# Linear attention feeding a gated causal convolution: a new instruction order, two more batches through the DMA crossbar, one load on another queue

## The chip, the cores and the metric

The kernel runs on one core of a Trainium2 chip. TensorE (PE), VectorE (DVE), ScalarE (ACT), GpSimd (POOL) and SyncE (SP) each work through their own list of instructions in order, and wait for one another by semaphores. SP computes nothing here; it issues DMAs. POOL computes and issues DMAs as well. The metric is the device time of one execution, in microseconds (us).

## The reference: what is computed

There are 8 batches, 8 heads, 576 positions and 64 features per head. With w_phi of 64 x 128:

```
phi(x): proj = x @ w_phi;  proj -= max|proj| over features;  [exp(proj), exp(-proj)]
kv = phi(k)^T v        z = sum over positions of phi(k)
x  = (phi(q) kv) / (phi(q) z + 1e-6)          heads side by side: 8 x 576 x 512
gate = sigmoid(causal convolution of x with 5 taps per channel)
out  = (gate * (x @ w_val)) @ w_out
```

## The kernel before

**Stages of a batch b.** The names below are the methods of the class Emit, and each of them is one task of the plan.

1. Load: `load` brings q and k of batch b as bf16 into one pair of tiles (KQN) that all batches from 2 on share. It is issued by POOL, q before k. `loadv` (line 504) brings v in fp32, issued by SP. Batch 0 comes in fp32 in nine pieces on SP (`load32`).
2. Transpose to features by rows: `xpose` (line 536) is a DMA transpose through the crossbar, issued by SP, for k and for q from batch 2 on. Batches 0 and 1 go through TensorE (`tp32`, `tp16`) and are copied out of PSUM by DVE or ACT.
3. k side: `kp` projects (PE), `kmax` takes the maxima (DVE), `kexp` the exponentials (ACT), `ek` the exponentials of the maxima (ACT), `vs` scales v by them (POOL, or DVE), `st` forms kv and z (PE), `kv` copies them out (DVE or ACT).
4. q side: `qm` projects for the maxima (PE), `qmax` (DVE), `mqt` and `mqr` transpose the maxima (PE, DVE), `rx` spreads them over a small identity (POOL, or DVE), `qp` projects again and adds them (PE), `qexp` (ACT).
5. `num` multiplies by kv (PE), `nrm` divides (DVE) into XN. The result is then transposed into XT: by 8 PE transposes (`xtp`, line 695) and a DVE copy (`xtc`, line 709) for each of two blocks, or, for the batches in `XB`, by a DMA transpose (`xtd`, line 706) that SP issues. A third, small block goes through PE always. `halo` (POOL) copies the positions that the convolution reaches back to.
6. `gate` (PE), `tanh` (ACT), `val` (PE), `gv` (DVE), `gvc` (POOL), `out` (PE), `oev` (ACT or DVE) and `odma` (SP).

q and k of batch 0 are kept in the second KTIL buffer and q and k of batch 1 in the second QTIL buffer, so the profile calls these transfers KTIL<-in_q_dram, QTIL<-in_q_dram and the like.

**What sets the order.** `build` lists 1,089 tasks with their dependencies. The kernel does no scheduling of its own: `ORDER` is a written-out table of task numbers, and each engine's instructions follow that table. `FLEX` names the engine of every task that has a choice, `BANKS` the PSUM banks. `WARM` puts dummy matmuls at given places of the order. Since every engine works in order, a task that waits holds up all that stands behind it on its engine. Two small POOL copies are there only to wait: `hold` keeps the loads of batch 1 back until a piece of batch 0 has landed, and `holdx` keeps the loads of batch b+2 back until the transposed q of batch b+1 has landed, since the KQN tiles are free only then.

**Queues.** SP issues, in order, the loads of batch 0, all v loads, one copy of the second half of w_val (`c_dup`, line 448), the transposes of k and q, the transposes of XN for the batches in XB, and the output. POOL issues the q and k loads and the weights. Both kinds of queue share the same 16 DMA engines.

Of the kernel before, what the change touches and what calls it, by code (L numbers as in the profile page):

```python
# [16 lines left out]
B, H, S, D = 8, 8, 576, 64  # L17
F = 128
DM = 512
P = 128  # L20
# [6 lines left out]
XB = (6, 7)  # L27
# [6 lines left out]
    "81:2:1 156:4:2 "  # L34
# [6 lines left out]
    "0 1 2 9 3 4 11 5 6 10 42 13 7 8 44 20 21 12 46 47 22 23 24 25 45 26 27 28 29 40 41 183 184 30 14 32 31 33 43 180 50 19 "  # L41
    "181 76 160 161 36 49 34 48 37 74 51 77 80 162 163 52 75 164 165 35 15 38 53 16 39 78 62 17 81 79 306 307 54 166 167 82 "
    "83 18 58 182 84 57 59 85 102 176 56 174 90 60 177 61 103 91 105 104 178 55 179 308 309 86 220 92 93 94 87 88 98 170 221 "
    "99 89 175 222 101 171 168 172 223 63 216 64 100 217 173 169 65 197 218 224 225 200 95 199 219 96 97 70 66 67 185 310 311 "
    "201 187 198 188 203 189 68 190 204 226 227 69 192 186 202 228 71 191 72 240 229 232 193 73 230 194 112 114 231 196 205 "
    "108 195 113 241 115 106 243 244 242 116 118 109 236 233 234 107 235 207 117 316 206 119 317 110 312 313 332 318 319 120 "
    "121 433 111 208 434 435 351 122 209 126 314 315 333 334 352 127 347 335 320 210 128 322 323 129 436 437 353 130 438 439 "
    "348 123 131 124 125 354 237 238 355 349 321 324 326 327 356 139 212 350 357 239 140 328 331 330 358 211 325 213 245 246 "
    "247 440 441 214 132 215 329 133 367 141 368 371 134 248 359 375 369 363 254 142 249 370 360 361 260 250 362 255 261 256 "
    "442 443 364 462 251 137 336 366 257 463 135 365 138 136 454 464 337 262 444 445 567 465 252 450 456 263 568 569 485 253 "  # L50
    "148 258 457 486 570 571 264 455 453 338 149 259 452 144 152 376 274 145 275 153 377 265 378 266 479 451 276 458 154 155 "
    "480 267 461 339 483 340 460 268 269 341 484 271 272 459 481 482 572 573 270 477 446 273 156 342 343 344 345 478 487 488 "
    "489 449 372 157 448 346 277 490 373 447 283 574 575 146 147 278 501 374 493 381 497 498 491 505 695 492 284 466 578 281 "
    "500 382 579 499 279 282 280 385 386 696 697 581 391 698 699 580 506 609 392 610 158 159 507 494 508 576 577 150 151 495 "
    "379 468 380 393 615 394 467 616 472 286 496 582 473 287 387 388 469 613 614 470 585 584 502 471 583 617 618 389 504 395 "
    "290 383 700 701 390 384 503 611 612 590 702 703 291 474 593 475 476 592 399 400 594 619 401 285 294 517 591 597 620 586 "
    "518 295 596 595 625 396 397 405 406 621 408 588 398 511 637 587 407 589 706 629 633 709 708 409 521 515 512 402 403 404 "
    "522 296 297 827 292 293 516 288 289 598 143 704 705 509 707 638 410 630 640 510 639 631 411 828 829 745 523 632 302 741 "
    "303 746 622 830 831 414 605 524 604 722 742 412 415 623 723 606 624 743 607 832 833 725 413 724 626 525 608 627 634 628 "
    "600 744 739 298 740 599 513 714 636 299 514 601 635 834 835 416 602 715 737 603 429 738 710 716 519 747 300 301 425 717 "  # L60
    "711 641 748 520 421 955 430 713 712 647 642 718 532 533 422 653 721 648 529 426 530 654 534 526 535 536 720 527 531 537 "
    "544 304 305 854 528 753 719 545 749 726 857 765 856 423 424 655 754 755 540 956 957 431 432 656 766 768 767 733 855 538 "
    "958 959 541 756 750 427 428 752 649 539 757 643 728 650 644 657 542 543 727 758 875 751 876 761 759 842 651 652 732 845 "
    "760 551 873 547 417 552 645 843 874 871 548 844 762 729 418 730 764 836 837 646 846 872 734 735 763 731 869 658 659 847 "
    "849 660 736 877 848 870 838 667 668 781 669 878 839 879 771 546 777 960 961 782 772 563 880 775 778 885 840 841 564 850 "
    "661 662 664 665 852 776 783 663 559 666 419 420 853 881 962 963 882 784 553 554 884 560 670 672 851 886 883 889 671 1005 "
    "673 674 1006 982 858 888 676 887 890 984 549 550 675 897 769 677 865 779 683 985 891 785 892 983 964 965 898 565 566 900 "
    "770 974 773 977 684 860 774 555 685 686 687 899 864 556 893 780 975 1001 557 558 795 688 796 786 1002 976 787 997 797 "
    "789 790 999 788 998 791 970 1003 1000 859 1004 792 973 793 794 972 800 966 969 679 1007 801 861 968 862 678 971 1008 798 "
    "967 863 680 894 978 561 562 802 895 799 1025 979 1009 1013 804 1021 896 803 805 1010 866 981 867 807 868 903 986 980 907 "  # L70
    "913 806 1011 1012 808 681 682 988 904 1022 1017 914 1023 992 1026 1027 915 908 691 916 987 909 823 993 689 690 1028 901 "
    "1024 809 810 692 910 994 1014 824 902 995 1016 1018 989 990 1015 819 1019 991 811 1020 996 1031 905 906 1035 693 694 "
    "1029 812 820 1032 917 815 1030 911 912 1037 927 1041 1036 928 924 1038 925 825 826 1042 921 1039 1040 929 1033 1034 922 "
    "1043 816 918 919 926 1044 930 920 936 932 813 814 923 931 1045 1049 933 1052 1055 1050 937 1046 1051 1047 1056 821 822 "
    "1053 1064 1048 934 1057 817 818 1062 1065 1060 935 1058 1054 943 1063 939 940 947 1059 1061 1067 1071 1079 951 1066 1075 "
    "938 944 945 946 948 941 942 1068 1083 1080 949 950 1072 1076 1084 1069 1070 1073 1074 1081 1082 1087 1088 952 953 954 "
    "1077 1078 1085 1086 "
)
FLEX = (
    "DDAAAAAAAAPPDPPDPDPPDDAAADDDDDDPPDPPDPPPPPAAADAPPAPPAPPPPDADDAPPAPPDPDPPPAAADDPPAPPAPPPPPADAAPPAPPDPPPPPADDADPPAPPDPPPPP"  # L80
    "ADDDPPDPDDPPPPPAAADA"
)
BANKS = (
    "616077010145236745674545234523450124567670101236704523011012367454523670102107662331012301236767014501012345567672345236"
    "723345453620167012301012345177032345456745232301010123670016723676723014672362067456745236767454012454567450101676767230"
    "101123456723012367101453226723670101236723762644545010123674567236767016016745230145015234570423674567016745014111456745"
    "452323010145670101023674567454501301670400167672301234501076602323452301234567010101015452323236745456767102301452345236"
    "7675427670145676745234523674501523670123452301450177670145236701230103162"
)


# [66 lines left out]
def build(plan, em=None):  # L158
# [7 lines left out]
    A = plan.add  # L166
    h = {}
    seq, oseq = [], {}

    def G(*k):  # L170
        return h.get(k)
# [690 lines left out]
```

## Time and profile before

| what | value |
|---|---|
| median of 3 runs | 227.13 us (225.67 to 228.78) |
| the profiled execution's own time | 227.83 us |
| its span, first to last instruction | 226.1 us |
| PE busy | 195.4 us (86%) |
| DVE, ACT, POOL busy | 177.4, 178.6, 136.8 us |
| DMA packets | 39.83 MB, mean 176 GB/s |
| TensorE clock granted, mean of the span | 0.985 |

The profile page cuts the span into 40 slices of about 5.65 us and gives each engine's busy share in tenths. Further views are the chain of work that ended last, the waits (who waited for whom), timelines of one engine, and windows (busy time between two points). Landing times of single DMAs are read from the trace's DMA completions. A wait is put down to the thing that came last.

### The profile page before, as it was taken

To read this page: it belongs to the slowest core of one execution; us is meant where nothing else is said; L and a number is where in the kernel's file an instruction comes from. 1 tells how busy PE (TensorE), PEld (TensorE's weight loads), DVE (VectorE), ACT (ScalarE), POOL (GpSimd) and SP (SyncE) were. 2 spreads that over 40 slices of the span, in tenths; PEclk is the share of its full clock that TensorE was granted. 3 is DMA by queue.
4 is the path that set the end of the run, shared out by engine and by line. 5 is a ranking of instruction groups with operands and counts; after the bars stand their busy time and mean duration, and the time that the engine had idled before them with its cause. 6 is when DMAs were issued, how large, how long until landed. Compare 5 with 4: busy or idle time off the path is not lost.

```text
span 226.1 us, 8730 instructions
## 1 busy us (share of the span) xinstructions
PE 195.4 (86%) x3768; PEld 141.2 (62%) x3787; DVE 177.4 (78%) x272; ACT 178.6 (79%) x264; POOL 136.8 (61%) x196
## 2 busy tenths in 40 slices
PE   3697677788979999889999998889999999899990
PEld 2474446566656766567776875566766867687630
DVE  3589999988978989977989878778988967653640
ACT  2599999989989999769999998868999997243230
POOL 4589988896279278928893089906693796010200
PEclk9979999999999999999999999999999999999997
DMA  6999986999989599949995979879932311954085
GB/s 219 292 277 283 215 171 110 243 210 174 130 217 246 119 173 264 253 76 181 255 259 106 161 218 232 213 114 203 259 100 83 96 46 40 154 102 138 0 249 169
DMA packets 49424, 39.83 MB, mean 176 GB/s; under 512 B 33706, under 2 KB 38826, under 8 KB 49322
## 3 DMA queue, kind: packets, MB, share of 16 engines
q1 hardware_dynamic: 43136, 29.63, 55.4%
q0 software_dynamic: 5760, 9.31, 23.1%
q8 instruction: 29, 0.48, 0.8%
q10 hardware_dynamic: 490, 0.35, 0.5%
q14 instruction: 9, 0.07, 0.1%
HBM read 30.49 MB, written 9.44 MB: 177 GB/s over the span
## 4 chain that ended last, share of the span: by engine, by line
PE 57%; DMA 14%; DVE 9%; POOL 8%; ACT 5%; issue 4%; SPq 0%; DVEq 0%; POOLq 0%; ACTq 0%
PE PS L775 12%; PE PS L751 10%; PE PS L594 7%; PE PS L733 6%; PE PS L551 6%; DMA qT<-KQN 6%; DVE MQP L558 4%; PE PS L671 4%; POOL VT L584 4%; POOL RX L637 3%; DMA kT<-KQN 3%; PE PS L739 3%; DMA KTIL<-in_q_dram 3%; DVE MK L558 2%; PE PS L700 2%
## 5 line engine op out<-in xcount | busy, mean ns | idle before, releaser
L568 ACT ACTIVATE KTIL<-PS 128x1024 bf16<-128x1024 f32 (+1 forms) x80 | 72.2, 967 | 4.9 <-PE PS L551 3.2
L584 POOL TENSOR_TENSOR VT<-VN,EK 128x1152 bf16<-128x1152 f32 x31 | 65.8, 2122 | 7.9 <-ACT EK L577 6.8
L658 ACT ACTIVATE QTIL<-PS 128x1024 bf16<-128x1024 f32 x64 | 62.4, 1052 | 4.3 <-PE PS L650 4.2
L637 POOL TENSOR_TENSOR RX<-MQR,ident 128x512 bf16<-128x512 bf16 (+1 forms) x36 | 34.5, 986 | 25.3 <-DVE MQR L630 18.4
L558 DVE TENSOR_REDUCE MK<-PS 128x8 f32<-128x1024 f32 (+1 forms) x40 | 44.3, 1112 | 5.0 <-PE PS L551 3.8
L558 DVE TENSOR_REDUCE MQP<-PS 128x8 f32<-128x1024 f32 (+1 forms) x40 | 43.6, 1112 | 4.0 <-PE PS L551 2.4
L751 PE MATMUL PS<-XT,WV 64*128 64x288 bf16 x512 | 35.1, 283 | 0.2 <-DVE MQP L558 0.2
L743 ACT ACTIVATE TH<-PS 128x576 bf16<-128x576 f32 x32 | 20.4, 661 | 16.7 <-PE PS L739 13.0
L757 DVE SCALAR_TENSOR_TENSOR GV<-TH,PS 128x576 bf16<-128x576 bf16 x32 | 23.8, 751 | 10.6 <-PE PS L751 8.1
L775 PE MATMUL PS<-WOUT,GV 128*128 128x512 bf16 x112 | 29.5, 380 | 1.0 <-issue 0.2
L751 PEld LDWEIGHTS <-WV 64*128 64x128 bf16 x512 | 25.1, 94 | 7.3 <-issue 2.2
L594 PE MATMUL PS<-VT,KTIL 64*128 64x65 bf16 x1152 | 23.2, 191 | 4.7 <-issue 2.8
L594 PEld LDWEIGHTS <-KTIL 64*128 64x128 bf16 x1152 | 21.0, 94 | 8.3 <-issue 5.0
L692 DVE TENSOR_TENSOR XN<-PS,RCP 128x512 bf16<-128x512 f32 x32 | 22.1, 692 | 2.2 <-DMA XT<-XN 1.1
L733 PE MATMUL PS<-XT,GF 128*64 128x288 bf16 x256 | 21.2, 289 | 1.9 <-issue 1.0
L671 PEld LDWEIGHTS <-QTIL 128*128 128x128 bf16 x512 | 17.8, 97 | 6.5 <-issue 4.0
L671 PE MATMUL PS<-KV,QTIL 128*128 128x65 bf16 x512 | 19.8, 194 | 0.8 <-ACT QTIL L658 0.8
L551 PE MATMUL PS<-W,kT 64*128 64x128 bf16 x288 | 15.2, 223 | 4.0 <-DMA kT<-KQN 1.4
L775 PEld LDWEIGHTS <-GV 128*128 128x128 bf16 x128 | 11.3, 98 | 11.4 <-issue 0.2
L608 ACT ACTIVATE OUTS<-PS 128x512 f32<-128x512 f32 x21 | 12.6, 613 | 5.4 <-PE PS L775 5.3
L551 PE MATMUL PS<-W,qT 64*128 64x128 bf16 x288 | 15.0, 219 | 2.0 <-ACT QTIL L658 0.8
L733 PEld LDWEIGHTS <-GF 128*64 128x64 bf16 x256 | 13.6, 109 | 4.4 <-issue 2.6
(77 smaller groups left out, 256.2 us busy)
## 6 DMA issues: line engine op xcount, KB each, us to landing
VN<-in_v_dram SPq DMA_DIRECT2D x8, 1152.0 KB, 8.3
out_dram<-OUTS SPq DMA_DIRECT2D x31, 256.0 KB, 3.2
KQN<-in_q_dram POOLq DMA_DIRECT2D x6, 576.0 KB, 8.9
KQN<-in_k_dram POOLq DMA_DIRECT2D x6, 576.0 KB, 11.9
KTIL<-in_k_dram SPq DMA_DIRECT2D x4, 288.0 KB, 4.0
KTIL<-in_q_dram SPq DMA_DIRECT2D x4, 256.0 KB, 5.8
out_dram<-OUTS SPq DMA_DIRECT2D x14, 64.0 KB, 2.7
QTIL<-in_q_dram POOLq DMA_DIRECT2D x1, 576.0 KB, 9.7
```

Source lines behind the costliest of these rows:

```text
L551: nc.tensor.matmul(self.PS[:, t.grp.banks[par], i * P:(i + 1) * P], X[rows, (c0 + i) * P:(c0 + i + 1) * P], self.W2[rows, :], start=True, ...
L558: self.nc.vector.tensor_reduce(o, self.two(t.grp, n * P).rearrange("p a (c f) -> p a c f", f=F), AX.X, ALU.max, apply_absolute_value=True)
L568: self.nc.scalar.activation(self.KTIL[b % 2][:, s, c0:c0 + n, :, :].rearrange("p c a f -> p a c f"), self.two(t.grp, n * P).rearrange("p a ...
L584: eng.tensor_tensor(self.VT[g][:, s, :, 0:D], self.VN[b % 2][:, NC * g:NC * g + NC, :], e.to_broadcast([P, NC, D]), ALU.mult)
L594: nc.tensor.matmul(self.PS[:, t.grp.banks[ab], (s * 2 + x) * E1:(s * 2 + x + 1) * E1], self.KTIL[b % 2][rows, s, J // 2, J % 2, :], self.V ...
L637: eng.tensor_tensor(self.RX[u][:, :, 0:n, :], m, e, ALU.mult)
L658: self.nc.scalar.activation(o, i, AF.Exp, scale=1.0 - 2.0 * s)
L671: nc.tensor.matmul(self.PS[:, t.grp.banks[h // 4], (h % 4) * E1:(h % 4 + 1) * E1], Q[:, s, c % 2, h, (c // 2) * P:(c // 2 + 1) * P], self. ...
L733: self.nc.tensor.matmul(self.PS[h2 * D:(h2 + 1) * D, t.grp.banks[par], 0:R], self.GF[:, h, i, :], X[:, h, :, HALO - 8 * s:HALO - 8 * s + X ...
L751: nc.tensor.matmul(self.PS[:, t.grp.banks[par], 0:R], self.WV2[rows, h, j * P:(j + 1) * P], X[rows, h, :, HALO:XW], start=(h == 0), stop=( ...
L757: nc.vector.scalar_tensor_tensor(out=self.GV[b % 3][:, j, :, :], in0=self.TH[j][:, :, :], scalar=1.0, in1=self.two(t.grp, R), op0=ALU.add, ...
L775: nc.tensor.matmul(self.PS[:, t.grp.banks[0], :], lhsT, self.WOUT[:, j, :], start=(j == 0), stop=(j == 3))
```

## The change

The diff has six parts.

1. `ORDER`, `FLEX` and `BANKS` are new tables (the planner that wrote them, which is no part of the kernel, took its transfer times from landings).
2. `XB` is (4, 5, 6, 7) where it was (6, 7): four more blocks of XN go through `xtd` on SP and no longer through `xtp` on PE and `xtc` on DVE. The dependency that made all `xtd` wait for the last k and q loads is gone.
3. `loadv` of batch 1 is issued by POOL, after the q and k loads and w_val; it was the second v load on SP, next to that of batch 0.
4. `hold` waits for the fifth piece of q of batch 0 (`HOLDU`); it waited for the fourth piece of k.
5. `WARM` places 1, 3 and 1 dummy matmuls where it placed 1 and 2.
6. By the new table POOL has 32 of the 40 `rx` (36 before) and 30 of the 32 `vs` (31 before); DVE has the others. DVE has 10 of the 16 `kv` (9 before) and 16 of the 36 `oev` that can go either way (14 before).

```
-XB = (6, 7)
+XB = (4, 5, 6, 7)
+HOLDU = 4
-    "81:2:1 156:4:2 "
+    "76:6:1 80:7:3 128:6:1 "
...
+                if w == "q":
+                    hold = [None, A("lk", b, 0, "POOL", 0.15, fn("hold", HOLDU), [lds[HOLDU]], rank=-600)]
...
-                if w == "k":
-                    hold = [None, A("lk", 0, 0, "POOL", 0.15, fn("hold", 3), [lds[3]], rank=-600)]
...
-        ld = h["lv0",] = A("lv", b, 0, "SP", 0.65, fn("loadv", b),
+        ld = h["lv0",] = A("lv", b, 0, "POOL" if b == 1 else "SP", 0.65, fn("loadv", b),
...
-                    xt = h["xtp", b, i] = A("xtp", b, i, "SP", 1.4, fn("xtd", b, i), nrms + war + [G("xf", B - 1)], lat=-0.2)
+                    xt = h["xtp", b, i] = A("xtp", b, i, "SP", 1.4, fn("xtd", b, i), nrms + war, lat=-0.2)
...
     def hold(self, t, u):
-        self.nc.gpsimd.tensor_copy(self.HOLD[:, :], self.XN32["k"][:, u * 9 * D:u * 9 * D + 1])
+        c = UNITS[u][0] * P
+        self.nc.gpsimd.tensor_copy(self.HOLD[:, :], self.XN32["q"][:, c:c + 1])
...
     def loadv(self, t, b):
-        self.nc.sync.dma_start(self.VN[b % 2][:, :, :].rearrange("p (hp j) d -> p hp (j d)", hp=4), self.rows("v", b))
+        eng = self.nc.gpsimd if t.eng == "POOL" else self.nc.sync
+        eng.dma_start(self.VN[b % 2][:, :, :].rearrange("p (hp j) d -> p hp (j d)", hp=4), self.rows("v", b))
```

The tables, decoded into task names, put the queues so at the places that matter (left before, right after; a number behind a name is the batch, then the unit):

```
POOL, start   hold, loadq1, loadk1, c_wv, loadq2, c_gt, loadk2, rx0 x3, vs0 x4, rx1 x5
         ->   hold, loadq1, loadk1, c_wv, loadq2, loadk2, loadv1, vs0, rx0 x2, vs0 x2, c_gt, rx1 x3
POOL, b 2     rx1 x5, vs1 x2, holdx2, c_wo, halo0, loadq3, loadk3, vs1 x2
         ->   rx1 x3, vs1 x2, holdx2, c_wo, loadq3, loadk3, halo0, rx1, vs1 x2, rx1
POOL, b 5     holdx6, rx5 x3, loadq7, vs5, loadk7, rx5, vs5, halo4, vs5, rx5, vs5
         ->   rx5 x2, holdx6, loadq7, rx5, loadk7, vs5 x3, gvc2, halo4, vs5     (two rx5 on DVE)
SP, start     loadv0, loadv1, c_dup, xposek2, xposeq2, loadv2
         ->   loadv0, xposek2, c_dup, xposeq2, loadv2
SP, b 4       odma1 x2, odma2 x3, loadv6, xposek7, odma2, xposeq7, odma3 x2, loadv7
         ->   odma1, odma2, odma1, xtd4, odma0, xtd4, xposek7, odma2, loadv6, odma2, xposeq7,
              odma3, xtd5, odma3, xtd5, odma2, loadv7
```

`c_gt` is the set-up of the convolution's weights, 16 POOL instructions; `c_wv` and `c_wo` load w_val and w_out.

## The prediction

> **What bounds the kernel now.** I read the page's busy times and slices first, then windows of 50 us, then the waits, and last the chain of work over the one stretch where it leaves TensorE for long. The page:
>
> ```profile
> PE 195.4 (86%) x3768; PEld 141.2 (62%) x3787; DVE 177.4 (78%) x272; ACT 178.6 (79%) x264; POOL 136.8 (61%) x196
> ...
> PE   3697677788979999889999998889999999899990
> ...
> DVE  3589999988978989977989878778988967653640
> ACT  2599999989989999769999998868999997243230
> ...
> DMA  6999986999989599949995979879932311954085
> ```
>
> PE is at seven tenths for the first eight slices (45 us), with DVE and ACT at nine; then it is at eight or nine tenths to the end. The windows put figures on the three bounds:
>
> ```profile
> 12.00:32.00 20.00, 15.95 (x262) 10.63 (x258) 19.23 (x24) 19.55 (x32) 19.73 (x27) 0.94 1.11 249
> ...
> 50.00:100.00 50.00, 44.54 (x967) 32.24 (x971) 44.08 (x65) 46.50 (x69) 32.84 (x40) 1.00 0.93 188
> 100.00:150.00 50.00, 46.65 (x948) 34.27 (x953) 41.76 (x63) 43.28 (x66) 33.09 (x48) 1.00 0.93 189
> 150.00:200.00 50.00, 48.17 (x979) 35.85 (x988) 41.21 (x71) 40.38 (x60) 28.40 (x36) 1.00 0.55 121
> ```
>
> (Columns: window, length, busy PE, PEld, DVE, ACT, POOL, granted clock, DMA share, GB/s.) From 12 to 32 us DVE and ACT leave 0.8 and 0.5 us of 20 unused: they set the pace, beside DMA engines that are full (1.11). From 50 to 200 us PE works 139.4 of 150 us, so 10.6 us is all that a better order can win there without taking work off PE. The DMA engines are nearly as full (0.93) until 150 us. The waits say why:
>
> ```profile
> SPq L539 <- DMA KQN<-in_k_dram: 67.5, 6, 15.6
> ...
> POOL HOLD L487 <- DMA qT<-KQN: 14.6, 5, 10.3
> ```
>
> Each of the six `xposek` waited for k to land. The cycle is: hold released, load q and k (12 us), transpose both (9 us), hold released again; the holds end at 44.8, 65.8, 85.6, 108.2 and 130.8 us, a period of 20 to 23 us, as long as PE needs for a batch. Where this cycle is late it shows in the chain of work:
>
> ```profile
> 124.77 5.89 DMA qT<-KQN
> ...
> 130.78 0.19 POOL HOLD L487
> ...
> 144.07 2.08 POOL VT L584
> ...
> 146.41 0.80 PE PS L594 x39
> ```
>
> POOL idled 10.31 us at this hold with all five `rx` of batch 5 behind it, then worked without a break until 146.4 us, and PE got the last `st` of batch 5 only then.
>
> **The change, part by part.** The sum is made against the profiled execution (227.83 us, span 226.1), 0.70 us above the median of 227.13; I take 0.7 off at the end.
>
> *Crossbar for batches 4 and 5.* Off PE go 4 blocks of 8 transposes. The group of such transposes is 7.4 us for 96, so 32 are 2.5 us; back to back a block takes 0.55 us in the chain. PE loses 4 x 0.55 = 2.2 us of work between 135 and 167 us, where it is 95% busy: **-2.2**. Off DVE go 4 copies of 0.685 us; DVE is not the bound there (41 of 50 us), so 0. On SP come 4 issues of 1.3 us; the queue has room, it waits 67 us in all. The new wait: each `xtd` waits for `nrm`, and behind it on SP stand `odma0`, `xposek7`, `loadv6`, `xposeq7`. Batch 4's last `nrm` ended at 136.9 us and `xposek7` could start only at 147.8, so these hold up nothing. Batch 5's have `loadv7` behind them, issued at 156.8 and first used after 181: covered. What is late next is `gate`. A transpose of XN landed 3.3 to 5.0 us after issue (median 4.1) with no loads beside it, and `nrm` is done 1.3 us after its `num` (163.64 to 164.92), which makes 5.4 us. In the new order the PE work between the last `num4` and the first `gate4` is two `qp` (0.6 each), four projections (0.35), three `out` (0.81) and half of `st5` (1.26): 6.3 us. Between the last `num5` and `gate5` it is 5.6 us. So quiet transposes would just fit; beside q and k of batch 7 the row nearest in kind is `xpose` beside loads, 6.3 to 6.8 us to landing with 2.25 times the bytes. Each of two batches may stall PE by 0 (4.1 us to landing) to 2.2 us (6.8 us: 8.1 against 5.9 of cover): **+1.5**, between 0 and +4.4, nearer to the small transposes' own row.
>
> *POOL in batch 5.* Two `rx5` now stand ahead of the hold, two more on DVE, and only one behind it. With the hold at the same time, the stretch from 130.8 to 146.4 us (5 `rx` of 1.04, 4 `vs` of 2.12 plus 0.27, 2 loads, a halo) loses 4 x 1.04 us and gains a `gvc` of 0.78: `st5` could come 3.4 us sooner. PE's own gaps from 138 to 151 us (0.58, 0.45, 0.52, 0.47, 0.59) are all there is to win, 2.6 us. I take half, **-1.3**, between -2.6 and 0, since DVE gets two `rx` (0.76 each) there.
>
> A row speaks against this part. When DVE did the one `vs` that it has (186.13 us, 1.44 us long), the small POOL cast beside it took 1.40 us in place of 0.26. The Trainium skill, page "SBUF — State Buffer" (section on practical consequences), has the rule: a DVE instruction with two SBUF inputs shuts out a GpSimd instruction that reads SBUF for its whole length. The trace agrees with it in that row. By it each `rx` or `vs` moved to DVE stops POOL while it runs, the two `rx5` cost POOL 1.5 of the 3.4 us, and the sum would be some 0.6 us higher.
>
> *Start.* Without v1 and batch 1 beside them the pieces of q0 follow k0 (landed at 7.0 us) at the rate of those first slices, 300 GB/s: 1.18 MB in 3.9 us. The second piece, which came at 10.17 us and cost ACT its 1.49 us idle, comes at about 8.7: -1.5. The hold now ends near 11 us where it ended at 7.05, and behind it on POOL are all seven loads. But the DMA engines have v0 to bring until 14 us, so they do not run dry. Nine tensors of 1.18 MB or nearly so took them from 3 to 33 us, 3.4 us each; k2, now the eighth of the nine and no longer the last, should land near 33 us where it landed at 35.2 (3 us, eight times 3.4, and some 2 us for stragglers), and v1 near 36, with `vs1` wanting it at 39.2. `c_dup` (7.0 us to landing) moves behind `xposek2`, to 44 us, before its first use at 51.9. So the first hold of the cycle ends 1 to 2 us sooner; `halo0`, now behind `c_wo` and two loads (0.8 + 0.5 + 0.75 us), eats that. `c_gt` (7.8 us of POOL) moves behind three `vs0` and is first needed by `gate0` at 46. Against it: DVE takes one `vs0` (1.44 + 0.27), one `rx0` (0.76) and two small copies (0.42 each) and gives up three of 0.7: +1.2 us; ACT takes a copy of 0.6, one like 0.97 and a `kv` of 0.61 for two of 0.42: +1.3 us. Both are full there, so these count: -1.5 + 1.3 and a little of the sooner hold, **-0.5**, between -3 (copies hidden, hold 2 us sooner and used) and +2 (q1 late by the later hold). Two more dummy matmuls (0.38 us each) lie in PE's idle time: 0; cover gone, +0.8.
>
> *The rest of the table.* Nearly every engine's list is permuted. Its planned ties can win some of the other 8 us of PE gaps or add as much; nothing in the trace prices it: 0, between -2.5 and +2.5. The tail (34 `out` matmuls, 7.5 us, then the last outputs) has the same work in another order: 0.
>
> Sum: -2.2 + 1.5 - 1.3 - 0.5 = -2.5, so 225.3 against the profiled execution and **224.6 us** against the median, 1.1% faster.
>
> **Rivals.**
> (a) *The cycle of loads becomes the bound at batch 7: slower.* Two `xtd4` now fall into the loads of q7 and k7, and `loadv6` moves from ahead of `xposek7` to between `xposek7` and `xposeq7`. From 189 to 198 us two transposes and five outputs took 6.8 us of DMA time; about 2 of it is outputs, so a transpose costs up to 2.4 us. Two of them and v6's 3.5 us ahead of `xposeq7` put its landing from 158.65 to 167 us. Its first use, `qm7`, ran at 160.24, and all of PE stands behind it: from 160.24 on each us is lost, 6.7 us. With -2.2 kept, and the 0.7: 227.83 + 4.5 - 0.7 = 231.6. I call it **232**. For it: DMA share near 1 from 128 to 144 us, only 1.6 us of slack. Against it: v6 leaves that stretch, which should bring k7 sooner by what the transposes cost.
> (b) *The order is simply better: faster.* The gates are not late, the 2.6 us at batch 5 and the 1.5 us at the start come in full with the copies hidden: -2.2 - 2.6 - 1.5 = -6.3, **220.8 us**. For it: POOL's stretch is real; against it, the cover of 5.6 to 6.3 us is no longer than the chain of 5.4.
> (c) *It does not do what it says*: v1 still shares all 16 engines, the gates take back the 2.2 us, and one wait replaces another: **227 us**. For it: the windows show DMA above 0.9 whatever queue issues. The Trainium skill, page "DMA: Bandwidth & Descriptors" (section "Issuing engines are not separate DMA queues"), says that too; the trace agrees, as q1's queue and POOL's ran together at a share of 1.11.
>
> **Chances.** Forecast 0.50, (a) 0.20, (b) 0.18, (c) 0.12. About 2% (4.5 us: 222.6 to 231.7) is what a measurement of this kernel can tell from no change; its three runs spread over 1.4%. Of the forecast's own range, 221.5 to 228, a tenth lies below 222.6, and of (b) nine tenths: 0.21 faster. Of (a) some nine tenths lie above 231.7: 0.18 slower. Within 2%: 0.61. The range for 8 in 10 takes in most of (a) and (b): 220.5 to 232.
>
> **What would show it.** In the profile after: 64 and not 96 transposes at the xtp line; `gate4` and `gate5` idle for XT<-XN by less than 2 us each; the hold of batch 6 with little idle time of `st5` behind it; ACT's wait of 1.49 us near 10.9 us gone; the first `xposek` before 35 us; `qm7` not waiting for qT. A long wait of PE for qT or kT in batches 6 or 7, or for XT, would make me wrong on the slow side; a PE share of 89% or more, on the fast side.

## The result, and the profile after

The changed kernel takes **237.7 us** (median; 236.57 to 241.85). The kernel before, run beside it on the same chip, takes 226.49. The ratio is 1.0462, with a 95% interval of 1.0352 to 1.0571: about 10.5 us slower. Medians here and below are of all executions of a version, while a ratio leaves out those that came out some per cent slow, and is against the kernel before timed beside that version. I had forecast 224.6 us, in a range from 220.5 to 232.

The profiled execution took 237.26 us with a span of 235.5. Its page, the same rows as before:

```profile
PE 198.8 (84%) x3739; PEld 140.5 (60%) x3757; DVE 193.1 (82%) x276; ACT 178.9 (76%) x262; POOL 134.9 (57%) x191
...
PE   3978576899998979999999908989999999899990
...
DVE  2799999899899899998999995879888889662641
...
PEclk9999979999999999999999965999999999999997
DMA  6999999796999899799959690799846036377076
```

PE has a zero in slice 24, from 135.4 to 141.3 us, where it had an eight or nine before; the clock that it is granted falls to 6 there and to 5 in the next slice. DVE is busy 15.7 us longer than before (177.4 to 193.1), although four copies of 0.685 us were taken from it. The windows, with the columns of those before (window, length, busy PE, PEld, DVE, ACT, POOL, granted clock, DMA share, GB/s):

```profile
12.00:32.00 20.00, 13.70 (x176) 8.73 (x177) 19.75 (x26) 18.40 (x30) 19.23 (x28) 0.98 1.12 233
50.00:100.00 50.00, 45.76 (x953) 32.61 (x957) 46.11 (x67) 46.43 (x70) 35.87 (x47) 1.00 0.94 186
100.00:150.00 50.00, 41.75 (x794) 30.26 (x792) 44.40 (x60) 36.47 (x56) 31.44 (x42) 0.90 0.78 157
150.00:200.00 50.00, 47.97 (x969) 33.26 (x976) 43.39 (x63) 44.06 (x65) 26.10 (x33) 1.00 0.68 157
```

Between 12 and 32 us PE does 2.3 us less work than before, and from 100 to 150 us 4.9 us less. The second is the larger loss, and the chain of work has it in one piece (start, length, what):

```profile
131.31 0.60 DVE RX L641
...
133.04 0.99 DVE RX L641
134.03 7.36 issue
141.38 0.75 DVE GV L761
142.18 0.40 PE PS L649 x2
...
142.78 1.92 PE PS L755 x16
```

A small DVE instruction, then 7.36 us in which DVE waits for nothing that the profile shows, then work goes on. The last row is a `val` group of 16 matmuls: 1.92 us instead of the 0.98 that such a group takes elsewhere in this chain, at the low clock after the stall (0.50 from 141.3 to 147.2 us). What DVE did in that time stands in its timeline (start, length, engine, line, operation, out<-in):

```profile
131.22 0.68 DVE L641 TENSOR_TENSOR RX<-MQR,ident 128x512 bf16<-128x512 bf16 x1
...
133.04 8.42 DVE L641 TENSOR_TENSOR RX<-MQR,ident 128x256 bf16<-128x256 bf16 x1
141.38 1.41 DVE L761 SCALAR_TENSOR_TENSOR GV<-TH,PS 128x576 bf16<-128x576 bf16 x2
```

The first row is `rx5,1`, the second `rx5,4`: half as large and twelve times as long. `rx` is the operation for which both inputs lie in SBUF. GpSimd beside it:

```profile
132.18 0.61 POOL L528 DMA_DIRECT2D KQN<-in_q_dram  x1 [0.22 <-issue]
132.81 1.05 POOL L641 TENSOR_TENSOR RX<-MQR,ident 128x512 bf16<-128x512 bf16 x1
133.80 0.81 POOL L528 DMA_DIRECT2D KQN<-in_k_dram  x1
134.63 2.13 POOL L588 TENSOR_TENSOR VT<-VN,EK 128x1152 bf16<-128x1152 f32 x1
136.69 0.27 POOL L589 CAST VT<-EK 128x18 bf16<-128x18 f32 x1
136.85 2.12 POOL L588 TENSOR_TENSOR VT<-VN,EK 128x1152 bf16<-128x1152 f32 x1
138.91 0.25 POOL L589 CAST VT<-EK 128x18 bf16<-128x18 f32 x1
139.07 2.11 POOL L588 TENSOR_TENSOR VT<-VN,EK 128x1152 bf16<-128x1152 f32 x1
141.13 0.45 POOL L589 CAST VT<-EK 128x18 bf16<-128x18 f32 x1
```

GpSimd works without a break through the loads of batch 7, one `rx` and three `vs` of batch 5. Only its last cast is longer than its fellows (0.45 against 0.26), and there `rx5,4` ends. So it looks as if DVE had been shut out by seven GpSimd instructions in a row. The waits about the load cycle, on which I had spent most of my worry, are not longer than before (of SyncE's six `xposek`, four wait last for k where all six did):

```profile
SPq L543 <- DMA KQN<-in_k_dram: 53.1, 4, 21.5
...
POOL HOLD L490 <- DMA qT<-KQN: 9.8, 2, 6.3
```

For the transposes of XN PE waits 0.2 us in all in this profile, once, at 213.5 us.

### The profile page after: what moved, and what is told of

Its sections match the earlier page's. It is cut to its first block, busy times and chain, and to the rows that moved or that the text cites. A ratio compares the mean times of both kernels' runs of the same rounds, so it can differ in the third digit from the quotient of the medians.

```text
span 235.5 us, 8674 instructions
## 1 busy us (share of the span) xinstructions
PE 198.8 (84%) x3739; PEld 140.5 (60%) x3757; DVE 193.1 (82%) x276; ACT 178.9 (76%) x262; POOL 134.9 (57%) x191
## 4 chain that ended last, share of the span: by engine, by line
PE 52%; DVE 22%; issue 8%; ACT 8%; DMA 7%; SPq 1%; DVEq 0%
PE PS L779 11%; PE PS L755 9%; PE PS L598 6%; PE PS L555 5%; PE PS L737 5%; PE PS L675 5%; ACT KTIL L572 4%; DVE MK L562 4%; DVE MQP L562 4%; DMA kT<-KQN 3%; DVE XN L696 3%; DVE RX L641 2%; PE PS L649 2%; PE PS L743 2%; DMA KTIL<-in_k_dram 2%
## 5 line engine op out<-in xcount | busy, mean ns | idle before, releaser
L588 POOL TENSOR_TENSOR VT<-VN,EK 128x1152 bf16<-128x1152 f32 x30 | 64.3, 2143 | 4.8 <-ACT EK L581 4.7
L641 POOL TENSOR_TENSOR RX<-MQR,ident 128x512 bf16<-128x512 bf16 (+1 forms) x32 | 31.0, 990 | 41.3 <-DVE MQR L634 26.3
L755 PE MATMUL PS<-XT,WV 64*128 64x288 bf16 x512 | 36.7, 290 | 0.1
L755 PEld LDWEIGHTS <-WV 64*128 64x128 bf16 x512 | 25.8, 96 | 7.3 <-issue 1.0
L675 PEld LDWEIGHTS <-QTIL 128*128 128x128 bf16 x512 | 18.5, 98 | 8.2 <-issue 6.4
L649 PE MATMUL PS<-qT,W 64*128 64x512 bf16 (+1 forms) x80 | 15.4, 368 | 8.0 <-DVE GV L761 7.1
L675 PE MATMUL PS<-KV,QTIL 128*128 128x65 bf16 x512 | 20.6, 195 | 1.6 <-DVE KV L606 1.0
L555 PE MATMUL PS<-W,qT 64*128 64x128 bf16 x288 | 15.5, 222 | 4.4 <-ACT KTIL L572 1.7
L779 PEld LDWEIGHTS <-GV 128*128 128x128 bf16 x128 | 11.3, 97 | 12.8 <-issue 1.7
```

Of the source, the lines that this page charges most:

```text
L555: nc.tensor.matmul(self.PS[:, t.grp.banks[par], i * P:(i + 1) * P], X[rows, (c0 + i) * P:(c0 + i + 1) * P], self.W2[rows, :], start=True, ...
L588: eng.tensor_tensor(self.VT[g][:, s, :, 0:D], self.VN[b % 2][:, NC * g:NC * g + NC, :], e.to_broadcast([P, NC, D]), ALU.mult)
L641: eng.tensor_tensor(self.RX[u][:, :, 0:n, :], m, e, ALU.mult)
L675: nc.tensor.matmul(self.PS[:, t.grp.banks[h // 4], (h % 4) * E1:(h % 4 + 1) * E1], Q[:, s, c % 2, h, (c // 2) * P:(c // 2 + 1) * P], self. ...
L755: nc.tensor.matmul(self.PS[:, t.grp.banks[par], 0:R], self.WV2[rows, h, j * P:(j + 1) * P], X[rows, h, :, HALO:XW], start=(h == 0), stop=( ...
L779: nc.tensor.matmul(self.PS[:, t.grp.banks[0], :], lhsT, self.WOUT[:, j, :], start=(j == 0), stop=(j == 3))
```

## The experiments

Theory S: the loss is `rx5,4` on DVE, shut out by GpSimd. Rival G: the crossbar's transposes beside the loads of batch 7 (a miss of my own term "+1.5"). Rival P: the start, where DVE got two-input work as well.

### One instruction to the other engine, in both kernels

```
 changed kernel, one letter of FLEX          (e1_rx54_pool)
-rx5,4: VectorE
+rx5,4: GpSimd
 kernel before, one letter of FLEX           (e3_before_rx52_dve)
-rx5,2: GpSimd
+rx5,2: VectorE
```

> The changed kernel with one task moved back: rx of batch 5, unit 4, runs on GpSimd and not on VectorE (one letter of FLEX). Theory S (shut out): in the changed kernel that instruction took 8.42 us on VectorE instead of 0.67 to 0.91, because GpSimd worked without a break beside it; VectorE, then TensorE, stood still for 7.1 us, and TensorE ran at a granted clock of 0.63 after it. S expects 8 to 10 us less than the changed kernel's 237.7: 227 to 230 us, no instruction of VectorE over 4 us between 125 and 150 us, and no TensorE wait over 2 us there. Theory G (gates, loads): the transposes on the crossbar and the order of the loads make TensorE late in batch 5 anyway, and the long instruction only fills a wait; then TensorE waits for XT or qT in its place and the time stays above 234 us.

Measured: 229.25 us, ratio to the kernel before 1.0115 (1.0056 to 1.0174). No stall of PE over 1.7 us is left in that stretch. By the ratios, 7.9 of the 10.5 us are gone with one letter.

> The kernel before with one task moved the other way: rx of batch 5, unit 2, on VectorE and not on GpSimd, at a place where GpSimd then works without a break from about 136 to 146 us. Theory S: the instruction is held up until GpSimd pauses, so it takes 4 to 10 us and not 0.76, and the time rises by 3 to 9 us to 230 to 236. A weaker form, S1 (VectorE waits for one GpSimd instruction at most): it takes up to 2.9 us, and the time is 226 to 229. Theory G: 0.8 to 1.5 us and 225 to 228.

Measured: 237.53 us, ratio 1.0444 (1.0315 to 1.0573). The kernel before, with nothing of the change in it but such a choice, is as slow as the changed one. Its DVE timeline:

```profile
133.08 9.45 DVE L637 TENSOR_TENSOR RX<-MQR,ident 128x512 bf16<-128x512 bf16 x1
```

PE stood for 8.45 us behind it. The stretch is the same: GpSimd had issued both loads of batch 7 and went on with `vs`, halo and `rx`. So S is shown from both sides, and G isn't needed for these 8 us. The unedited changed kernel, run once more, had the long wait again:

> The changed kernel once more, without any edit, to see whether the 8.42 us of the one instruction, and the 7.1 us of TensorE's wait behind it, are of this program or of one execution. S expects both again within 1 us; chance (a semaphore or a transfer that came late once) expects another place or none.

Measured: 239.24 us, `rx5,4` 8.68 us, PE idle 7.38 us behind it.

### All two-input work off DVE, and the start

```
 changed kernel                              (e2_no_dve_two_input)
-all 8 rx and 2 vs of VectorE
+on GpSimd
 changed kernel                              (e5_start_pool_too)
-rx5,4, rx0,3, vs0,1,0: VectorE
+rx5,4, rx0,3, vs0,1,0: GpSimd
```

> The changed kernel with all eight rx and both vs that VectorE had put on GpSimd, so that no instruction of VectorE with two inputs from SBUF runs beside GpSimd after the set-up. Theory S: the eight and two instructions took 17.4 and 5.5 - that is 15.9 us of VectorE for rx and 5.5 us for vs - where 6.0 and 2.9 would be their undisturbed price; without them the time falls to 225 to 229 us, as e1 or up to 2 us below it, if the start (2.5 us late at 40 us) was late for the same reason. If GpSimd's extra work (some 8 rx of 1.04 and 2 vs of 2.4, 13 us) is on the path, it is 1 to 4 us above e1. Theory G: above 234 us.

Measured: 229.55 us, ratio 1.0186 (1.0100 to 1.0271): no better than one letter. At the start GpSimd then has too much, and the first `gate0` is 6 us late in its profile. Off DVE isn't a remedy by itself.

> The changed kernel with rx of batch 5 unit 4 on GpSimd, as in the first experiment, and also rx of batch 0 unit 3 and the first batch's vs that VectorE had taken. Theory S at the start: these two took 1.90 and 2.20 + 1.06 us on VectorE, which is what TensorE waits for from 21 to 45 us, where 0.76 and 1.71 were their undisturbed price; GpSimd was idle for 2 us there. S expects the maxima of batch 1 (36.2 us in the changed kernel, 32.2 before) by 33 to 34 us and 226 to 228 us in all. Rival P (GpSimd becomes the bound of the start, its weights' set-up coming 3.4 us later, as in the second experiment where gate of batch 0 came at 53 us): 229 to 231 us, gate of batch 0 still 4 us or more later than before.

Measured: 228.67 us, ratio 1.0002 (0.9939 to 1.0064): the same as before. By the medians of all executions it is 0.5% slower (228.67 against 227.44). So besides the long wait there is probably a second, smaller loss from the two-input work that DVE got at the start: 1.1% or 2.6 us by the ratios (1.0115 to 1.0002), 0.7% or 1.5 us by the medians. The intervals of the two ratios overlap, so it is likely and not shown. In the changed kernel's profile the two that this run moves took 1.90 us (`rx0,3`) and 2.20 plus 1.06 us (`vs0` with its cast), and `mqt1`, the transposed maxima of batch 1, started at 36.1 us where the kernel before had it at 32.0; here it starts at 34.5, later than the 33 to 34 that S expected. Rival P falls: `gate0` starts 1.2 us later than before (47.5 against 46.3) and not four. What is left of the change, better start of transfers, crossbar and table, is worth nothing together that could be measured.

To see the transfers at the start alone, the kernel before got them:

```
 kernel before                               (e8_before_start)
-hold on a piece of k0; loadk2 behind c_gt; loadv1 on SyncE
+hold on the fifth piece of q0; loadk2, loadv1 on GpSimd ahead of c_gt
```

> The kernel before with another part alone: hold waits for the fifth piece of q of batch 0, and GpSimd issues k of batch 2 and then v of batch 1 ahead of the set-up of the weights (v of batch 1 no longer on the sync engine's queue). All else in the old order. My prediction expected qT of batch 2 1 to 2 us sooner than 44.7 us, ScalarE's 1.49 us wait near 10.9 us gone, and so 0 to 1.5 us less: 225 to 227 us. Rival H (the loads of batch 1 come too late behind the hold, 11 us instead of 7): q and k of batch 1 hold up TensorE near 20 to 25 us, 228 to 230 us.

Measured: 228.07 us, ratio 1.0045 (0.9997 to 1.0092): no gain. The transfers came as early as I had worked out, or earlier (k2 landed at 32.6 us and v1 at 36.6 here, at 29.2 and 32.6 in the changed kernel's trace), qT of batch 2 came 2.6 us sooner (42.1 against 44.7), and ScalarE's wait of 1.49 us is gone. It brought no time. Of rival H a part is seen: PE waits 1.8 us once for q of batch 1.

### The crossbar

```
 kernel before                               (e6_before_crossbar)
-XB = (6, 7)
+XB = (4, 5, 6, 7)
 e5's kernel, same places                    (e10_pe_transposes)
-XB = (4, 5, 6, 7)
+XB = (6, 7)
```

> The kernel before with one part of the change: the eight blocks of batches 4 and 5 that went through TensorE and VectorE (two per batch, four in all) go through the crossbar; all else in the old order. If TensorE's 2.2 us count and the gates wait little: 224 to 226 us (1 to 2 us under the kernel before). Theory G (the transposes land late beside the loads): gate of batch 4 or 5 waits for XT by 2 us or more, and the time is 227 to 230 us.

Measured: 237.68 us, ratio 1.0494 (1.0394 to 1.0595). The transposes were issued where the copies had stood in the order. Half of G is right: the order of the kernel before puts the transposes of batch 4 beside the loads of batch 7. They were issued at 137.08 and 139.26 us and landed at 145.18 and 150.53, after 8.1 and 11.3 us. But no wait of PE for these two is seen: `gate4` started at 150.66, right behind them, and the 3.02 us for which PE stood just before lie inside `st5`, in a row that the profile puts down to "issue" (last section). The other long wait, 3.01 us ahead of `gate5`, is the old order's: the second transpose of batch 5, whose block was ready at 160.5 us, stood on SyncE's queue behind the first, which waited for its own block until 169.6, and behind an output. After each of the two PE worked at a low granted clock (0.55 from 150 to 155 us, 0.50 from 175 to 181).

> The kernel of the fifth experiment (changed, with three tasks on GpSimd) with the crossbar for batches 6 and 7 only: the four blocks of batches 4 and 5 are again 8 TensorE transposes and a copy of VectorE each, at the same places of the order. If the crossbar wins its 2.2 us of TensorE time, this is 1.5 to 2.5 us slower than the fifth experiment: 230 to 231 us beside its 228.7. Theory F: the transposes delay what TensorE needs from the DMA engines; in the fifth experiment TensorE stood still for 2.2 us at 147 us with no semaphore to wait for, and a packet of the instruction queue started 2.4 us before it went on. Then the gap is under 1 us here and the two times agree within 1 us.

Measured: 233.91 us, ratio 1.0318 (1.0224 to 1.0412), 5.2 us over e5 by the medians and 7 by the ratios. Theory F, with its times within 1 us, falls. 2.5 us is PE's time for the 32 transposes. Another 2.7 us in the profile are waits of PE for DVE's copies of them (0.9, 0.8, 0.8 and 0.2 us), which the new order left no room for. So the crossbar is worth more in this order than my 2.2 us, but the order was made for it, and this doesn't say what the best order with PE transposes would give.

### What makes the wait long

Every kernel here has two-input instructions of DVE beside GpSimd, and nearly all wait for one GpSimd instruction or none: 0.4 to 3.3 us. The question was what makes it eight. First, the load between:

```
 changed kernel                              (e7_loadk7_last)
-rx5,0, loadk7, vs5, vs5, vs5
+rx5,0, vs5, vs5, vs5, loadk7
```

> The changed kernel with one move: GpSimd issues the load of k of batch 7 after the three vs of batch 5 and not between its rx and them. VectorE's rx of batch 5 unit 4 then starts beside GpSimd's rx with no DMA issue of GpSimd before the chain of three vs. Theory S2 (a GpSimd DMA issue between two of its instructions is what lets VectorE miss its turn): the instruction takes 0.7 to 2.5 us, as the other rx of VectorE beside GpSimd's. Theory S3 (any unbroken run of GpSimd shuts VectorE out): it takes 6 to 8 us as before. The time itself may be anything from 228 to 240 us, since k of batch 7 comes some 8 us later.

Measured: 236.57 us, `rx5,4` still 7.77 us. It isn't the load between. Next, by itself:

> The disputed price by itself. This kernel computes nothing of the reference (it writes zeros): twice over, six stretches in which VectorE starts one rx-like instruction (512 elements of bf16, two inputs from SBUF) beside GpSimd's second of several instructions. GpSimd runs: plain, two rx and three vs; load, the same with a load of q issued by GpSimd just before; mid, with a load of k between the rx and the vs; real, with both, as in the changed kernel; hw, with a load of v issued by the sync engine; rx, nine rx in a row. Theory S3 (any unbroken run shuts VectorE out): 6 to 9 us in all six. Theory S2 (loads issued by GpSimd bring it about): 0.7 to 2.3 us in plain, hw and rx, 5 us or more in load, mid and real. Theory S1 (one GpSimd instruction at most): under 2.5 us in all.

Measured: 1.44 us without a load ahead (plain, mid, hw, rx), 3.51 us with one ahead and 4.34 us with one ahead and one behind, the same to 0.01 us both times. None of the three theories had these numbers: an issued load matters, but not for 8 us. Both loads away from the spot, in the kernel:

```
 changed kernel                              (e11_loads7_behind_vs5)
-loadq7, rx5,0, loadk7, vs5, vs5, vs5, gvc2
+rx5,0, vs5, vs5, vs5, loadq7, loadk7, gvc2
```

> The changed kernel with both loads of batch 7 on GpSimd's queue (q7 and k7) moved behind the three vs5 that follow rx5,0; rx5,4 stays on VectorE. In every traced case so far in which VectorE's two-input instruction missed more than one GpSimd instruction, GpSimd had issued a load 0.6 to 2.8 us before it; where the last load was over 3.2 us back, or none was, it waited for one instruction at most (up to 3.3 us with its own time). Theory L (a load just issued makes VectorE miss its turn): rx5,4 now takes 0.7 to 3 us, TensorE's stall behind it is under 2.5 us, and the kernel comes to 228 to 231 us, as with rx5,4 on GpSimd (229.25). Theory R (the unbroken run of GpSimd instructions is enough): rx5,4 takes 5 to 8 us still, and the kernel 234 to 238 us. The loads of batch 7 land some 8 us later than in the changed kernel's profile; in the run with k7 alone moved that cost nothing that showed, and I expect 0 to 1 us.

Measured: 237.69 us, ratio 1.0455 (1.0331 to 1.0579). The time fits theory R and the instruction fits theory L. In its DVE timeline `rx5,4` is short:

```profile
132.79 0.68 DVE L641 TENSOR_TENSOR RX<-MQR,ident 128x256 bf16<-128x256 bf16 x1
```

and PE has a new wait, the first row of its list (in all, times, longest):

```profile
PE PS L737 <- DMA XT<-XN: 7.8, 1, 7.8
```

The loads went out at 140.0 and 140.6 us instead of 132.2 and 133.8, and the second transpose of batch 4, issued at 140.2, landed at 152.8, after 12.6 us. One collision was traded for the other. In the changed kernel the shut-out had held this one off: its transposes were issued at 147.6 and 149.8 us, after the loads, and landed in 3.1 and 3.6.

I then tried to move the loads past both, one place further:

```
 changed kernel                              (e13_loads7_behind_halo4)
-loadq7, rx5,0, loadk7, vs5, vs5, vs5, gvc2, halo4
+rx5,0, vs5, vs5, vs5, gvc2, halo4, loadq7, loadk7
```

> The changed kernel with the two loads of batch 7 on GpSimd's queue moved one place further than in the run before, behind halo4, which waits for the crossbar transposes of batch 4; rx5,4 stays on VectorE. Theory GL (a load that GpSimd has just issued makes VectorE miss its turns, and a load in flight stretches the crossbar's transposes; there is a place free of both): rx5,4 takes 0.7 to 2.5 us, the two transposes of batch 4 land 3 to 5.5 us after their issue instead of 3.1 and 12.6 us, and gate4 waits under 1.5 us for them. The loads then go out 6 to 8 us later than where VectorE isn't shut out, and SyncE's queue holds the transposes of batch 7 and the v of batch 6 behind them; that may cost 0 to 5 us. In all 228 to 234 us. Rival H (the 12.6 us were not the loads' doing): a transpose of batch 4 still takes over 8 us, and the kernel comes to 235 us or more.

Measured: 236.23 us, ratio 1.0524 (1.0435 to 1.0613); `rx5,4` 2.29 us; the transposes 3.1 and 11.3 us. My expectation rested on an error: `halo4` copies columns of the third block, which goes through PE, and doesn't wait for the crossbar. The loads went out at 141.2 us, again into the transposes. So it repeats e11 and leaves rival H untested. What the traces do show is when such transposes land. With no load beside them they took 3.1 to 3.6 us (batch 4 in the changed kernel). Issued near the end of the loads they took 4.0 to 5.0 (e1, e5, e15). In all seven runs with the load of k7 in flight, the first transpose that met it landed 0.5 to 1.1 us after k7 had landed: it looks as if it had waited for the load to end.

What decides the length came out of two small programs that compute nothing of the reference.

> No part of the reference is computed: the outputs are zeros, and the time is no kernel's. Eight stretches, twice over. In each, VectorE does one two-input instruction (rx, 128x512, or 128x256 where it is called short) that starts beside a GpSimd rx, behind which come four vs of batch size (2.1 us each, and a small cast). What differs is what GpSimd issued before: (1) nothing; (2) a load of 576 KB just before; (3) the same, short rx; (4) the load, then two rx (2 us) before; (5) the load, then five rx (5 us) before; (6) a load just before and a second one behind the rx, short; (7) a load just before, beside a load of 1152 KB on SyncE's queue, short; (8) all of these, short. Theory L (a load just issued makes VectorE miss turns): (1) and (5) 1.2 to 1.7 us; (2), (3) and (4) 3 to 6 us; (6) at least as long. Theory T (it misses them until the load's transfers are through): as L, but (7) and (8), where other transfers stretch the load, are longer than (3) and (6) by 2 us or more, 6 to 10 us, as in the kernel. Theory R (neither; the earlier microbenchmark's 3.5 and 4.3 us were chance of alignment): no order by loads, and (1) as often long as the others.

Measured: 1.43 to 1.51 us without a load. With one, 3.24 to 3.52 us, whether it was issued 0.9 or 5.9 us earlier, landed or not, beside other traffic or not; 4.08 us with the second load behind. L's order by loads holds, but not its "just issued": the stretch with the load 5.9 us back is as long as the others. T falls too: neither the load's age nor its transfer counts.

> No part of the reference is computed: the outputs are zeros. Eight stretches, twice over; in each VectorE's two-input rx (128x256) starts beside a GpSimd rx, and a run of GpSimd instructions follows. (1) no load, run of four vs with casts; (2) a load just issued, same run; (3) as 2, but GpSimd waits once for VectorE between its load and its rx; (4) as 2, but GpSimd waits for the load's landing; (5) no load, run of four vs without casts; (6) a load, same run; (7) no load, run of eight rx; (8) a load, run of eight rx. Theory W (VectorE misses its turns as long as GpSimd has gone on without a wait since its load): (1), (5) and (7) 1.1 to 1.5 us, (2) 3.2, (3) and (4) 1.1 to 1.5 us; (6) and (8) show where VectorE gets in: if the cast behind a vs is what lets it in, 6 to 10 us in (6) and (8); if it is the second or third place between two instructions, 3 to 5.5 us. Rival L (a load of the last few microseconds, whatever GpSimd waited for): (3) is as long as (2), 3.2 us, and (4), where the load is through, 1.1 to 1.5 us.

Measured, from DVE's timeline, the eight stretches of the first round in order (the second round agrees to 0.06 us):

```profile
2.92 1.11 DVE L90 TENSOR_TENSOR RXD<-M,ID 128x256 bf16<-128x256 bf16 x1
...
13.89 9.88 DVE L90 TENSOR_TENSOR RXD<-M,ID 128x256 bf16<-128x256 bf16 x1
...
26.01 1.17 DVE L90 TENSOR_TENSOR RXD<-M,ID 128x256 bf16<-128x256 bf16 x1
...
41.98 1.18 DVE L90 TENSOR_TENSOR RXD<-M,ID 128x256 bf16<-128x256 bf16 x1
...
52.53 1.17 DVE L90 TENSOR_TENSOR RXD<-M,ID 128x256 bf16<-128x256 bf16 x1
...
62.86 9.46 DVE L90 TENSOR_TENSOR RXD<-M,ID 128x256 bf16<-128x256 bf16 x1
...
73.05 1.17 DVE L90 TENSOR_TENSOR RXD<-M,ID 128x256 bf16<-128x256 bf16 x1
...
83.05 9.13 DVE L90 TENSOR_TENSOR RXD<-M,ID 128x256 bf16<-128x256 bf16 x1
```

That is the whole effect by itself. With a load and then an unbroken run (2, 6, 8) DVE waits for all of the run, four `vs` or eight `rx`: 9.1 to 9.9 us. The same load and the same run with one wait of GpSimd in between (3, 4): 1.2 us. The same run without a load (1, 5, 7): 1.1 to 1.2 us. Theory W holds, though it had expected 3.2 us in (2), and L falls. It also throws light on the 3.2 to 4.3 us of e9 and e12: there each `vs` wrote the tile that the one before had written, and so had to wait for it, and DVE got in one instruction ahead of such a `vs`. That reading is argued, not shown.

Last, in the kernel, with nothing moved and one instruction of 0.2 us added:

```
 changed kernel, vs, ahead of the first vs5   (e15_gpsimd_waits_for_rx54)
+        if (b, g, s) == (5, 1, 1):
+            nc.gpsimd.tensor_copy(self.HOLD[:, :], self.RX[4][:, 0, 0, 0:1])
```

> The changed kernel with nothing moved: loads, rx5,4 on VectorE and the run of vs5 stay where they are. One instruction is added: behind the load of k7 and ahead of the first vs5, GpSimd copies one element of what VectorE's rx5,4 writes, and so stands still until VectorE has had its turn. Theory W (VectorE gets its turn as soon as GpSimd stands still once after its loads; the 8 us are nothing else): rx5,4 takes 1.2 to 2.2 us, TensorE has no stall over 2.5 us there, the loads of batch 7 are through before the crossbar's transposes of batch 4 go out, and the kernel comes to 227.5 to 230 us, as with rx5,4 on GpSimd (229.25). Rival (rx5,4 on VectorE costs by where it stands among VectorE's other work, or the loads of batch 7 collide with something whatever VectorE does): 232 us or more.

Measured: 228.21 us, ratio 1.0105 (1.0044 to 1.0165). GpSimd's timeline has the wait, 1.51 us of standing still (line numbers are two higher behind the added lines):

```profile
133.14 1.05 POOL L643 TENSOR_TENSOR RX<-MQR,ident 128x512 bf16<-128x512 bf16 x1
134.13 0.80 POOL L528 DMA_DIRECT2D KQN<-in_k_dram  x1
136.44 0.18 POOL L588 COPY HOLD<-RX 128x1 bf16<-128x1 bf16 x1 [1.51 <-DVE RX L643]
136.58 2.11 POOL L590 TENSOR_TENSOR VT<-VN,EK 128x1152 bf16<-128x1152 f32 x1
```

and DVE's has both `rx`, the first behind GpSimd's `rx`, the second free:

```profile
132.78 1.98 DVE L643 TENSOR_TENSOR RX<-MQR,ident 128x512 bf16<-128x512 bf16 x1
...
135.88 0.43 DVE L643 TENSOR_TENSOR RX<-MQR,ident 128x256 bf16<-128x256 bf16 x1
```

So 8.1 us by the ratios (9.5 by the medians) come with this one wait, the low clock behind it included. The 1.05% that stays has the size of the start's likely loss (e1 against e5). No version came out faster than the kernel before; the nearest, e5, equals it.

## Why the prediction was wrong

**POOL in batch 5 (-1.3, between -2.6 and 0): the step that failed.** I moved four `rx` off GpSimd's unbroken stretch and priced the two that DVE got at 0.76 us each, the mean of two rows (0.69 and 0.83 us). In one of them GpSimd had issued a load 0.5 us before, but DVE came first; in neither did GpSimd run on behind a load while DVE waited. One of them took 0.68 us, the other 8.42, and PE stood 7.12 us behind it and then worked at a granted clock of 0.63 (mean from 140 to 150 us). The bound of 0 on the upper side was wrong: it assumed that what GpSimd is given less to do can cost nothing elsewhere.

I had the rule in hand and used it one way round only. I wrote that a DVE instruction with two SBUF inputs shuts out GpSimd, and that the sum would be some 0.6 us higher by it, which I did not add. The Trainium skill, page "SBUF — State Buffer" (section "Who interferes with whom"), says that whichever issues first has the ports and the other is blocked; so the row of 186 us that I quoted, where GpSimd's cast grew to 1.40 us, has a mirror image in which DVE is the one that grows. The traces agree with that: all but the long rows of `rx` in these kernels waited for one GpSimd instruction at most, 3.3 us with their own time. They go beyond it too: the page gives the lock for one instruction, and DVE waited for up to nine. The row that I quoted, first DVE, then GpSimd:

```profile
186.13 1.44 DVE L584 TENSOR_TENSOR VT<-VN,EK 128x1152 bf16<-128x1152 f32 x1
...
186.31 1.40 POOL L585 CAST VT<-EK 128x18 bf16<-128x18 f32 x1
```

The gain that this step was to bring did not come either. With the wait gone (e5), the last `st5` ends at 149.8 us, 1.6 us later than before and not sooner: PE has a gap of 2.2 us in it (below).

**Start (-0.5, between -3 and +2).** The transfers were right (first `xposek` at 29.3 us, ACT's wait of 1.49 us down to 0.71), but sooner transfers brought nothing (e8: 0 to +2 us). The term I mis-sized is DVE's: one `vs0` at 1.44 + 0.27 and one `rx0` at 0.76 us took 2.20 + 1.06 and 1.90 us beside GpSimd, with both at 19.75 and 19.23 of 20 us busy. By e1 against e5 the start cost some 1.5 to 2.6 us, about my upper end.

**Crossbar (-2.2 and +1.5).** PE waited 0 for the transposes of batches 4 and 5 in the changed kernel, and also in e1, e5 and e15, so the +1.5 was too much here; the PE work that I had counted ahead of `gate` covered them. In the changed kernel that is in part luck: the shut-out held the transposes of batch 4 back until the loads were through. And my upper end, 2.2 us for each batch, was much too low for the case beside loads: 8.1, 11.3, 12.6 and 11.3 us to landing where I had bounded it at 6.8, and waits of PE of 7.8 and 6.5 us (e11, e13). The row that I took the bound from was misread: each `xposek` waits until k has landed, as I wrote myself, so none of these rows had a load of q or k beside it.

**The rest of the table (0).** With the costly DVE work at both places out, the whole change is worth 0 (e5, within 0.6% either way), where crossbar and POOL come to -2.0 in my sum: the -1.3 that did not come accounts for most of it. Within what can be measured, 0 was right.

**The rivals.** (a) gave about the right direction for the wrong place: `qm7` was not held up, and the load cycle waited no longer than before. None of my rivals was a DVE that can't get its inputs, although the rule for it stands in the prediction's own text.

## What to carry to other kernels

A DVE instruction with two inputs in SBUF has no price of its own beside a busy GpSimd: look at what GpSimd does there. If GpSimd has issued a DMA and then goes on without having to wait for anything, DVE may wait for the whole run; give that instruction to GpSimd, or let GpSimd wait for DVE's result once (one copied element took 8 us off this kernel).

Price a crossbar transpose by what flies beside it: here 3 to 5 us for 256 KB with no load beside it, 8 to 13 us when two loads of 576 KB had gone out up to 4 us before, and 4 to 5 us at the end of these loads. Such a transpose landed about when the load did, so ask when the loads are through. When a fix lets a transfer start sooner, ask what it now flies beside, as e11 shows.

## What the runs showed of the hardware that I had not expected

The long shut-out itself: 9.1 to 9.9 us in six stretches out of six, and 1.1 to 1.2 us in ten others that differ by a load or by one wait. Why an issued load makes the difference, and why DVE gets in just ahead of the last cast of a run and not of the first, stays open.

PE has gaps in long rows of `st` that the profile puts down to "issue". The row where PE goes on, in the kernel before and in e5:

```profile
147.68 0.70 PE L594 MATMUL PS<-VT,KTIL 64*128 64x65 bf16 x33 [0.47 <-issue]
```

```profile
149.07 0.20 PE L598 MATMUL PS<-VT,KTIL 64*128 64x65 bf16 x2 [2.22 <-issue]
```

In the traces of the fourteen kernel runs there are 30 such gaps of over 0.4 us on PE, in `st` and elsewhere, and each ended 2.2 to 2.8 us after the start of a 16 KB packet on the instruction queue (among them before: 145.27 to 147.68; e1: 148.31 to 150.67; e5: 146.71 to 149.07; e6: 147.50 to 149.87). The Trainium skill, page "Advanced Engine Details and Errata" (section "ISA Cache"), gives lines of 16 KB or 256 instructions, which agrees with the packet's size. The gaps put down to "issue" add up to 4.1 us in the kernel before and 5.2 in e6, to 2.1 in e10 and 3.7 in e5, so each pair has more of them with the crossbar; but the changed kernel, which has the crossbar as well, has 2.2 and in its second trace 1.1. That they come with the packet is seen; that the transposes delay it is not shown.
